# Weight pieces joined during attention, a third early unit, squares on another engine: one core of Trainium2

## The chip, the cores and the metric

The kernel runs on one core of a Trainium2 chip. The core has five engines with instruction queues of their own: TensorE (PE in the profile; its weight loads are PEld), VectorE (DVE), ScalarE (ACT), GpSimd (POOL) and SyncE (SP), which here only issues DMA transfers. Each engine works its queue strictly in order; semaphores tie the queues together. The metric is the device time of one launch in microseconds; lower is better. The inputs are float32 arrays in DRAM, and the output must agree with a float32 reference.

## The reference, cut to what matters

```python
# attention: batch 4, 12 heads, 448 positions, head size 64
scores = einsum('bhij,hg->bgij', (q @ k.T) / 8, w_pre)      # mix the heads
attn   = exp(scores - max); attn /= attn.sum() + 1e-9
out    = einsum('bhij,hg->bgij', attn, w_post) @ v          # mix the heads again
x = out as 1792 tokens x 768
h = ((x @ w1) * (x @ w2)) @ w3 @ w_out                      # 768 -> 1024 -> 1024 -> 768
h = relu(h @ w_in) ** 2 @ moe2_w_out                        # 768 -> 2048 -> 768
```

The weights reach the device as 64-bit words, two 32-bit halves for each element.

## The kernel before, in words

**Attention.** The scores are worked in 16 groups of query rows, cut into 180 blocks of up to 120 rows (10 queries times 12 heads). The loop of the main body runs over steps `d`, two blocks to a step. `attention_step` (L455) emits each step's work for each engine: premix (TensorE, line L295, tile `sp`), rowmax (VectorE, L301, `nm`), exp (ScalarE, L309), 1/sum, the high and the low fp16 part of the probabilities (L334 on ScalarE, L341 on VectorE, `ph` and `pl`), the second head mix one or two steps later (L351, `tp`), its copy out of PSUM (L364, L366, `p`), and the product with v (L392, `pv`). The scores of the next group (L269, `sc`) are worked in the same steps, up to step 82; the premix of the last two blocks is in step 89, the last two `pv` in step 92. SyncE regroups the rows of each block two steps ahead by DMA (`r<-s`, L287). The `sp` tile has two PSUM buffers, so a premix waits until exp has read the block two earlier.

**Weights.** A float32r matmul works on a high and a low part of weights and data, three matmuls to a product (`mm3`, L58). `Weights` holds the path of one piece (128 x 384 or 128 x 512). `load` is a DMA by SyncE, of 64-bit words ("wide", 384 KB for 384 columns) or of plain float32 (half of that). A wide piece then needs `narrow` (one ScalarE operation, L89) and `join` (three VectorE operations, L101, L103, L105), which make the float32 value `f`. Every piece needs `place`, `high` (ScalarE, L121) and `rest` (GpSimd or VectorE, L125), which make `wh` and `wl`. `keep` (L510) writes the joined float32 back to DRAM (`w1f` and so on), from ScalarE's DMA queue, since the second half of the tokens reads the same weights again.

**The layers after attention.** `Moe` runs the first 896 tokens (half 0, t = 0 and 1 of 448 tokens) by a list of units: 16 `l1` units (w1 and w2 by turns, two pieces each, L679), between the first 12 of them the 16 pieces of `w_out`, then `p34`, the last four `l1`, `ly`, `l3` (relu and square, L746) and `l4`. `stage` (L514) moves the pieces along, some places ahead of the unit that TensorE works. Half 1 (L1009) works by a product scheme with seven products for eight in `stream`, with `gate` and `square` (L990) as the ends of a stream, and between the streams the `y1` units and the `l4_1` units of two token blocks each. Its order is a list of events with planned times: a term that is planned at T + 3.6 is emitted then, and each engine's queue has the order of emission.

**Between the two.** At step 82 (`closed`) the pool of attention's first half is released. `tail_plan` (L540) hands out loads of x (L636, 0.7 MB each in rows of 880 or 912 bytes), their splitting (L644: ScalarE high, GpSimd low part), and the first eight pieces of w1 and w2, by block number from step 82 on; what is left over is emitted after the last step. `early` (L561) works t = 0 of the first two `l1` units in three PSUM banks that the scores leave, six groups of three matmuls each, one group at the very end of the loop (from block 187) and the rest behind it. Before, all 36 of these matmuls run behind the last `pv`.

Of the kernel before, what the change touches and what calls it, by code (L numbers as in the profile page):

```python
# [10 lines left out]
F = mybir.dt.float32  # L11
# [3 lines left out]
AF = mybir.ActivationFunctionType  # L15
# [11 lines left out]
PW = 512  # L27
# [8 lines left out]
def fused_kernel(ctx, tc, q, k, v, w_pre, w_post, w1, w2, w3t, wo, win, wo2, eye, out):  # L36
# [366 lines left out]
            eng.dma_start(xd[n // 4, :, 3 * y : 3 * y + 3, o : o + ic], u[:, :, :ic])  # L403


    TAIL = {"w": 5, "ws": 2, "w8": 13, "n": 4, "x": -1, "xs": 2, "xn": 4, "xt": 2, "h": 7, "hn": 1}

    def attention_plan():
        ev = {}

# [69 lines left out]


    class Moe:
        def __init__(self, wp):
            self.w = Weights(wp, PW, 4, 2, 4, 8, 8)
            self.wp = wp
            wp.tile([128, 24], F, tag="pad", name="pad")
            self.xy, self.acc, self.ready, self.serial = {}, {}, set(), 0
            self.wot = {}
            l1 = [self.l1(m, s) for m in range(8) for s in range(2)]
            wop = [self.wo_piece(c, h) for c in range(8) for h in range(2)]  # L490
            mixed, rest = l1[:4] + wop[:6], wop[6:]
            for i in range(8):
                mixed.append(l1[4 + i])
                for _ in range(1 + (i % 4 == 3)):
                    mixed.append(rest.pop(0))
            assert not rest
            self.units = mixed + [self.p34(m) for m in range(8)] + l1[12:]
            self.units += [self.ly(n) for n in range(6)]
            for gr in range(2):
                self.units += [self.l3(8 * gr + f) for f in range(8)]  # L500
                self.units += [self.l4(gr, e) for e in range(6)]
            self.pieces = [s for ss, *_ in self.units for s in ss]
            n = np.cumsum([0] + [len(ss) for ss, *_ in self.units])
            self.at = [int(x) for x in n]
            self.order = [(2, 0), (3, 0), (0, 1), None, (1, 1), None, (2, 1), None, (3, 1)]
            for i in range(10, len(self.units)):
                self.order += [(i, t) if self.units[i][1] else None for t in range(len(self.units[i][0]))]
            self.events, self.clock = [], -sum(self.units[it[0]][2] for it in self.order if it)

        def keep(self, i):  # L510
            if i in self.w.ft and self.pieces[i].get("keep") is not None:
# [28 lines left out]
        def tail_plan(self):  # L540

            w, ev = self.w, {}

            def at(t, f):
                ev.setdefault(t, []).append(f)

            for i in range(11):
                t = TAIL["w"] + TAIL["ws"] * i if i < 8 else TAIL["w8"] + i
                at(t, lambda i=i: w.load(i, self.pieces[i]["src"], self.pieces[i]["wide"]))
                if i < 9:  # L550
                    at(t + TAIL["n"], lambda i=i: w.narrow(i))
                if i < 8:
                    for part in range(3):
                        at(t + TAIL["n"] + 1 + part, lambda i=i, part=part: w.join(i, part))
                    at(t + TAIL["n"] + 4, lambda i=i: (w.place(i), w.high(i), self.keep(i), w.rest(i)))
            for u in range(4):
                at(TAIL["x"] + TAIL["xs"] * u, lambda u=u: self.load_x(u))
                at(TAIL["x"] + TAIL["xn"] + TAIL["xt"] * u, lambda u=u: self.split_x(u))
            return ev

        def early(self, i, psum):  # L561
# [10 lines left out]
        def begin(self, ap_):  # L572
            self.ap = ap_
            self.load_x(4)
            slots = []
            for i in range(3):
                t = self.six(1, f"wox{i}")
                slots += [t[:, c, :HC] for c in range(6)]
            slots += [ap_.tile([128, TB], R, tag="oa", name=f"woa{i}", bufs=12)[:, :HC] for i in range(12)]
            t = ap_.tile([128, HT], R, tag="bh", name="wob", bufs=8)  # L580
            slots += [t[:, :HC], t[:, TB : TB + HC]]
            for c in range(8):
                for h in range(2):
                    self.wot[c, h] = slots[4 * c + 2 * h], slots[4 * c + 2 * h + 1]
            for u in (5, 6, 7):
                self.load_x(u)
            for i in range(2):
                self.units[i][1](None, 0, slice(0, TB), self.acc[i])

        def run(self, ps):  # L590
# [155 lines left out]
        def l3(self, f):  # L746
            def run(ws, t, ts):
                yh, yl = self.xy["y", t]
                if t == 0:
                    self.xy["h", f] = self.big(f"h0_{f}")  # L750
                hb = self.xy["h", f]
                acc = self.psum(f"l3_0_{f}_{t}")
                mm3(acc, [(self.chunk(ws, c), (yh[:, c], yl[:, c])) for c in range(6)])

                def done():
                    r = self.tmp(f"r0_{f}_{t}")
                    nc.scalar.activation(r, acc, AF.Relu)
                    self.split_chain(hb, ts, r, (0.8, lambda: nc.vector.tensor_tensor(r, r, r, ALU.mult)))

                self.chain((3.6, done))  # L760

            return self.source("win", f, 0, HC), run, 3.6
# [227 lines left out]
        def square(self, f):  # L990
            def finish(q, block, z, bank):
                i = f + 2 * q + (block[1] == "2")
                ts = slice(0, TB) if block[2] == "1" else slice(TB, HT)
                if ("h1", i) not in self.xy:
                    self.xy["h1", i] = self.big(f"h1_{i}")
                dst = self.xy["h1", i]
                if bank is not None:
                    nc.scalar.activation(z, bank, AF.Relu)
                    self.split_chain(
                        dst, ts, z, (0.9, lambda: nc.gpsimd.tensor_tensor(z, z, z, ALU.mult)), (0.4, lambda: None)  # L1000
                    )
                else:
                    self.split_chain(
                        dst, ts, z, (0.7, lambda: nc.vector.scalar_tensor_tensor(z, z, 0.0, z, ALU.max, ALU.mult))
                    )

            return finish

        def half1(self):  # L1009
# [3 lines left out]
            D = {}  # L1013
            for n in (0, 3, 1, 4, 2, 5):
                ws = self.plain_weights(T, self.w34_source(n))
                for t in range(2):
                    def go(cs, n=n, t=t, ws=ws):
                        ts = slice(t * TB, t * TB + TB)
                        if 0 in cs:
# [32 lines left out]
                    self.event(T, lambda go=go: go(range(6)))  # L1052
                    self.event(T + 3.6, lambda go=go: go((6, 7)))
                    T += 4.8
                    self.event(T + 0.1, after)
            for gr in range(2):
                T = self.stream(
                    T, [(wf["win"][8 * gr + f], wf["win"][8 * gr + f + 1]) for f in range(0, 8, 2)],
                    lambda: D["y"], self.square(8 * gr), self.tmp,
                )  # L1060
                for e in range(6):
                    o = 1024 * gr
                    ws = self.plain_weights(T, [wf["wo2"][e, :, o + PW * i : o + PW * i + PW] for i in range(2)])
                    for t in range(2):
                        def go(cs, gr=gr, e=e, t=t, ws=ws):
                            ts = slice(t * TB, t * TB + TB)
                            if 0 in cs:
                                D["o", gr, e, t] = self.psum(f"l4_1_{gr}_{e}_{t}")
                            mm3(D["o", gr, e, t], [
                                (self.chunk(ws(), c), tuple(x[:, ts] for x in self.xy["h1", 8 * gr + c])) for c in cs  # L1070
                            ], 0 in cs, 7 in cs)

                        self.event(T, lambda go=go: go((0, 1, 2, 3, 4, 6)))
                        self.event(T + 3.6, lambda go=go: go((5, 7)))
                        T += 4.8
                        self.event(T + 0.1, lambda gr=gr, e=e, t=t: self.l4_out(D["o", gr, e, t], 1, gr, e, t))

    with tc.manual_schedule(), ExitStack() as base:
# [29 lines left out]
        A.setup_pre()  # L1108
        step = iter(range(-5, (first[16] + 5) // 2 + 2))
        closed = (first[15] - RG) // 2  # L1110
        M, tail = None, {}
        for d in step:
            attention_step(A, d, ev)
            if d == -1:
                A.setup_post()
            if d == closed:
                sa.close()
                M = Moe(pool(sa, "wp"))
                tail = M.tail_plan()
                heads = (x for i in range(2) for x in M.early(  # L1120
                    i, lambda i: ps.tile([128, TB], F, tag="sc", name=f"e{i}", bufs=3)
                ))
            for g in (2 * d, 2 * d + 1):
                for a in tail.pop(g - 2 * closed - 1, []):
                    a()
                for _ in range(TAIL["hn"] if g >= nb + TAIL["h"] else 0):
                    next(heads, None)
        for u in sorted(tail):
            for a in tail[u]:
# [61 lines left out]
```

## Time and profile before

| | before |
|---|---|
| median of three runs | 1346.34 us (1346.01 to 1347.26) |
| the profiled execution, device time | 1348.09 us |
| its span in the trace | 1346.3 us |
| busy in the span | PE 1296.7 us (96%), DVE 865.1 (64%), ACT 703.4 (52%), POOL 476.0 (35%) |
| mean granted TensorE clock | 0.985 |
| moved by DMA | 191 MB, 142 GB/s on the mean |

Attention takes the first 466 us of the span, half 0 the stretch to about 950 us (its end overlaps the start of half 1's preparation on VectorE), half 1 the rest. "Busy" is the time in which an engine executes; TensorE's matmuls overlap, so their durations in a timeline add up to more than their starts are apart. PEclk is the share of TensorE's full clock that was granted. A row of the waits view names who waited, for whom, how long in total, how often, and the longest.

### The profile page before, as it was taken

What the parts mean: (1) busy time and instruction counts of PE and PEld (TensorE: products, weight loads), DVE (VectorE), ACT (ScalarE), POOL (GpSimd) and SP (SyncE); (2) the same over time, 40 slices, a digit from 0 to 9 for tenths busy, and PEclk for the clock granted to TensorE, in tenths of its full rate; (3) what the DMA queues carried; (4) which work ended last, traced back from release to release, by engine and by line L of the source; (5) the groups of instructions that cost most, each with busy time, mean ns of one, the idle gap of its engine ahead of it and who ended that gap; (6) DMA issues with size and microseconds to landing.
All of it is one profiled execution on the core that took longest, in us unless ns stands there. A gap on an engine that the chain in (4) does not pass through costs nothing. (4 is left out here: it accounts for less than half of the span.)

```text
span 1346.3 us, 23524 instructions
## 1 busy us (share of the span) xinstructions
PE 1296.7 (96%) x8714; PEld 1120.9 (83%) x8714; DVE 865.1 (64%) x1446; ACT 703.4 (52%) x1518; POOL 476.0 (35%) x481
## 2 busy tenths in 40 slices
PE   6999999999998799899999999999999999899998
PEld 3677777777776688899999989989999999899988
DVE  4898788888787788865247884888254426602821
ACT  5878878878886455543223443444345335423520
POOL 4243253244222222101332232210588458624730
PEclk8999999999999799999999999999999999999989
DMA  6565476466545567765266764576211211220221
GB/s 187 169 185 176 135 212 184 130 184 197 139 125 170 151 197 213 214 196 162 73 188 189 240 198 148 131 232 213 96 47 56 79 55 48 68 74 25 71 71 58
DMA packets 106423, 191.31 MB, mean 142 GB/s; under 512 B 22021, under 2 KB 73221, under 8 KB 105861
## 3 DMA queue, kind: packets, MB, share of 16 engines
q1 hardware_dynamic: 86437, 167.42, 42.5%
q10 hardware_dynamic: 19872, 22.39, 4.7%
q8 instruction: 69, 1.13, 0.4%
q14 instruction: 45, 0.37, 0.1%
HBM read 115.46 MB, written 35.78 MB: 112 GB/s over the span
## 5 line engine op out<-in xcount | busy, mean ns | idle before, releaser
L125 POOL TENSOR_TENSOR wl<-f,wh 128x384 fp32r<-128x384 f32 (+1 forms) x76 | 84.3, 1110 | 298.4 <-ACT wh L121 282.7
L295 PE MATMUL sp<-r,kpre 120*120 120x448 f32 x360 | 158.6, 563 | 7.4 <-DMA r<-s 5.5
L309 ACT ACTIVATE p<-sp,nm 120x448 f32<-120x448 f32 x180 | 113.5, 638 | 69.9 <-DVE nm L301 69.0
L301 DVE TENSOR_REDUCE nm<-sp 120x1 f32<-120x448 f32 x180 | 108.1, 619 | 43.1 <-PE sp L295 36.8
L351 PEld LDWEIGHTS <-ph 120*128 120x128 f16 (+1 forms) x1440 | 107.9, 99 | 29.0 <-issue 28.5
L324 POOL TENSOR_SCALAR sm<-sm 120x2 f32<-120x2 f32 (+3 forms) x94 | 31.4, 334 | 273.8 <-ACT p L309 265.0
L351 PE MATMUL tp<-kwh,ph 120*128 120x120 f16 x720 | 121.4, 219 | 3.7 <-DVE p L366 2.4
L341 DVE SCALAR_TENSOR_TENSOR pl<-p,sm,ph 120x448 f16<-120x448 f32 x180 | 124.2, 730 | 0.0
L351 PE MATMUL tp<-kwh,pl 120*128 120x120 f16 x720 | 120.6, 218 | 1.0 <-DVE pl L341 1.0
L351 PE MATMUL tp<-kwl,ph 120*128 120x120 f16 x720 | 120.7, 218 | 0.0
L334 ACT ACTIVATE ph<-p,sm 120x448 f16<-120x448 f32 x180 | 111.8, 681 | 16.1 <-DVE sm L329 13.3
L269 PE MATMUL sc<-kt,qh 128*110 128x448 f32 (+1 forms) x192 | 101.3, 528 | 9.1 <-DVE kt L230 7.6
L295 PEld LDWEIGHTS sp<-r,kpre 120*120 120x120 f32 x360 | 59.0, 184 | 49.1 <-issue 21.5
L280 ACT ACTIVATE s<-sc 110x448 f32<-110x448 f32 (+1 forms) x186 | 90.2, 553 | 9.2 <-PE sc L269 7.5
L366 DVE TENSOR_SCALAR p<-tp,iv 112x480 f32<-112x480 f32 (+1 forms) x135 | 90.9, 701 | 3.0 <-PE tp L351 2.7
L121 ACT ACTIVATE wh<-f 128x384 fp32r<-128x384 f32 (+1 forms) x104 | 58.2, 559 | 60.5 <-DVE f L105 52.5
L101 DVE TENSOR_SCALAR f<-y 128x384 int32<-128x384 int32 (+1 forms) x120 | 71.7, 598 | 23.4 <-ACT y L89 23.4
L392 PE MATMUL pv<-p,v 112*64 112x110 f32 (+1 forms) x1536 | 84.9, 269 | 1.8 <-DVE p L366 1.2
L103 DVE SCALAR_TENSOR_TENSOR f<-y,f 128x384 int32<-128x384 int32 (+1 forms) x120 | 81.5, 679 | 4.0
L105 DVE SCALAR_TENSOR_TENSOR f<-raw,f 128x384 int32<-128x384 int32 (+1 forms) x120 | 79.9, 666 | 4.1
L392 PEld LDWEIGHTS pv<-p,v 112*64 112x64 f32 x1536 | 77.9, 142 | 5.3 <-ACT y L89 1.4
L269 PE MATMUL sc<-kt,ql 128*110 128x448 f32 (+1 forms) x192 | 75.1, 391 | 2.6 <-POOL ql L252 1.9
(981 smaller groups left out, 3522.2 us busy)
## 6 DMA issues: line engine op xcount, KB each, us to landing
r<-s SPq DMA_DIRECT2D x172, 210.0 KB
raw<-w SPq DMA_DIRECT2D x32, 384.0 KB
raw<-win SPq DMA_DIRECT2D x32, 384.0 KB
raw<-wo SPq DMA_DIRECT2D x24, 512.0 KB
kraw<-k SPq DMA_DIRECT2D x22, 448.0 KB
raw<-w3t SPq DMA_DIRECT2D x16, 512.0 KB
qraw<-q SPq DMA_DIRECT2D x36, 220.0 KB
raw<-wo SPq DMA_DIRECT2D x16, 384.0 KB
```

What stands on the lines that cost most here:

```text
L103: nc.vector.scalar_tensor_tensor(fi, yi, -0x80000000, fi, ALU.bitwise_and, ALU.bitwise_or)
L125: eng.tensor_tensor(self.out[i][1], self.ft.pop(i), f32(self.out[i][0]), ALU.subtract)
L269: nc.tensor.matmul(sc[:ic], t[:, hh * ic : hh * ic + ic], self.kt[b, h // 2][:, h % 2], start=(i == 0), stop=(i == 1))
L280: nc.scalar.activation(self.st[n][:ic, h], self.sc.pop((n, h))[:ic], AF.Copy)
L295: nc.tensor.matmul(t[:kk], self.kpre[:kk, :kk], self.rt.pop(g)[:kk], start=True, stop=True)
L301: nc.vector.tensor_reduce(nm[:kk], self.sp[g][:kk], AX.X, ALU.max, negate=True)
L309: nc.scalar.activation(p[:kk], self.sp.pop(g)[:kk], AF.Exp, bias=self.nm.pop(g)[:kk], accum_out=self.sm[g // 2][:kk, g % 2 : g % 2 + 1],)
L334: nc.scalar.activation(self.phl[g % NP][0][:kk, :S], self.pt[g][:kk], AF.Copy, scale=self.sm[g // 2][:kk, g % 2 : g % 2 + 1])
L341: nc.vector.scalar_tensor_tensor(l, self.pt.pop(g)[:kk], self.sm[g // 2][:kk, g % 2 : g % 2 + 1], h, ALU.mult, ALU.subtract)
L351: nc.tensor.matmul(t[:, j, :, :cnt], p[:kk, j * JP : j * JP + 128], w[:kk, :, :cnt], start=(i == 0), stop=(i == 2))
L366: nc.vector.tensor_scalar(d, t, self.iv[:JP], None, ALU.mult)
L392: nc.tensor.matmul(t[64 * e : 64 * e + 64, x, :ic], self.v[b][:, j, g], self.p2[n][:, j, g, :ic], start=(j == 0), stop=(j == JC - 1),)
```

## The change

Four things. (1) The `Moe` object is made before the loop. Its new method `ahead` takes the first 24 pieces that have a `keep` (all pieces of the first 12 `l1` units), and spreads their load, narrow, join and store over attention's steps: one piece every three steps from step 4, with two buffers for each kind of tile in attention's first pool; loads and stores are issued by SyncE. In the unit list these 24 pieces then are plain float32 from DRAM. (2) `tail_plan` is denser: loads of the first eight pieces one per block, x loads and splits one per block. `early` now works three units, one group per block from block 175 on, and the unit (2, 0) leaves the list. (3) The squares of `l3` (VectorE before) and of half 1's C21 block (GpSimd before) become a ScalarE `Square` behind the relu. (4) In half 1 the first `y1` unit and the first `l4_1` unit of each group work token block 1 ahead of block 0, and the two terms that are held back to T + 3.6 are chosen to match.

```diff
     class Moe:
-        def __init__(self, wp):
-            self.w = Weights(wp, PW, 4, 2, 4, 8, 8)
...
-            self.order = [(2, 0), (3, 0), (0, 1), None, (1, 1), None, (2, 1), None, (3, 1)]
+            self.order = [None, (3, 0), (0, 1), None, (1, 1), None, (2, 1), None, (3, 1)]
...
+        def ahead(self, ka, n, start, period):
+            w, ev = Weights(ka, PW, 2, 2, 2, 0, 0), {}
...
+            for j, i in enumerate([i for i, x in enumerate(self.pieces) if "keep" in x][:n]):
+                d, x = start + period * j, self.pieces[i]
+                at(d, lambda i=i, src=x["src"]: w.load(i, src, True))
+                at(d + 2, lambda i=i: w.narrow(i))
+                for part in range(3):
+                    at(d + 3 + part // 2, lambda i=i, part=part: w.join(i, part))
+                at(d + 6, lambda i=i, dst=x["keep"]: store(i, dst))
+                self.pieces[i] = {"src": x["keep"], "wide": False}
+            return ev
...
             for i in range(11):
-                t = TAIL["w"] + TAIL["ws"] * i if i < 8 else TAIL["w8"] + i
+                t = 1 + i if i < 8 else 13 + i
                 at(t, lambda i=i: w.load(i, self.pieces[i]["src"], self.pieces[i]["wide"]))
-                if i < 9:
-                    at(t + TAIL["n"], lambda i=i: w.narrow(i))
+                if i == 8:
+                    at(t + 4, lambda i=i: w.narrow(i))
                 if i < 8:
-                    for part in range(3):
-                        at(t + TAIL["n"] + 1 + part, lambda i=i, part=part: w.join(i, part))
-                    at(t + TAIL["n"] + 4, lambda i=i: (w.place(i), w.high(i), self.keep(i), w.rest(i)))
+                    at(t + 4, lambda i=i: (w.place(i), w.high(i), w.rest(i)))
             for u in range(4):
-                at(TAIL["x"] + TAIL["xs"] * u, lambda u=u: self.load_x(u))
-                at(TAIL["x"] + TAIL["xn"] + TAIL["xt"] * u, lambda u=u: self.split_x(u))
+                at(u - 1, lambda u=u: self.load_x(u))
+                at(u + 3, lambda u=u: self.split_x(u))
...
                 def done():
                     r = self.tmp(f"r0_{f}_{t}")
                     nc.scalar.activation(r, acc, AF.Relu)
-                    self.split_chain(hb, ts, r, (0.8, lambda: nc.vector.tensor_tensor(r, r, r, ALU.mult)))
+                    nc.scalar.activation(r, r, AF.Square)
+                    self.split_chain(hb, ts, r)
...
                     nc.scalar.activation(z, bank, AF.Relu)
-                    self.split_chain(
-                        dst, ts, z, (0.9, lambda: nc.gpsimd.tensor_tensor(z, z, z, ALU.mult)), (0.4, lambda: None)
-                    )
+                    nc.scalar.activation(z, z, AF.Square)
+                    self.split_chain(dst, ts, z)
...
-                for t in range(2):
+                held = []
+                for t in ((1, 0) if n == 0 else (0, 1)):
...
-                    for t in range(2):
+                    for t in ((1, 0) if e == 0 else (0, 1)):
...
-                        self.event(T, lambda go=go: go((0, 1, 2, 3, 4, 6)))
-                        self.event(T + 3.6, lambda go=go: go((5, 7)))
+                        late = (5, 7) if t == 0 else (4, 6)
+                        self.event(T, lambda go=go, late=late: go([c for c in range(8) if c not in late]))
+                        self.event(T + 3.6, lambda go=go, late=late: go(late))
...
+        M, tail = Moe(), {}
+        ahead = M.ahead(ka, 24, 4, 3)
         for d in step:
             attention_step(A, d, ev)
+            for a in ahead.get(d, ()):
+                a()
...
-                heads = (x for i in range(2) for x in M.early(
+                heads = (x for i in range(3) for x in M.early(
...
-                for _ in range(TAIL["hn"] if g >= nb + TAIL["h"] else 0):
+                for _ in range(1 if g >= nb - 5 else 0):
                     next(heads, None)
```

## Rows read from the trace of the kernel before

**Rows 1.** Windows view, stretches: length, busy us of each engine (instructions), clock, DMA.
```profile
66.80:120.40 53.60, 53.46 (x570) 39.80 (x569) 49.38 (x86) 42.79 (x103) 23.61 (x28) 1.00 0.61 184
...
294.60:321.40 26.80, 26.11 (x269) 18.80 (x266) 24.32 (x46) 21.01 (x50) 15.30 (x17) 1.00 0.59 185
53.40:401.80 348.40, 346.45 (x3657) 257.29 (x3656) 293.76 (x549) 283.34 (x673) 118.81 (x154) 1.00 0.57 165
```
**Rows 2.** Windows view of later stretches: PE, PEld, DVE, ACT, POOL, clock, DMA.
```profile
475.00:575.00 100.00, 92.94 (x452) 84.28 (x453) 87.67 (x162) 52.77 (x105) 18.31 (x18) 0.98 0.72 209
750.00:950.00 200.00, 195.97 (x971) 181.20 (x970) 149.60 (x228) 88.29 (x175) 45.49 (x40) 1.00 0.62 194
1150.00:1300.00 150.00, 143.79 (x687) 131.89 (x686) 59.18 (x77) 54.12 (x108) 77.33 (x64) 0.97 0.19 60
441.00:456.60 15.60, 11.00 (x124) 8.57 (x125) 14.75 (x26) 8.92 (x20) 5.00 (x6) 0.76 0.57 142
```
**Rows 3.** Windows view, short stretches with a lowered clock, the same columns.
```profile
565.00:569.00 4.00, 4.00 (x16) 4.00 (x15) 3.90 (x8) 1.21 (x2) 0.00 (x0) 0.57 0.71 240
1172.00:1177.00 5.00, 4.47 (x14) 4.04 (x15) 0.48 (x1) 1.58 (x3) 2.14 (x2) 0.66 0.17 57
1285.00:1293.00 8.00, 7.43 (x21) 6.33 (x22) 1.71 (x2) 1.84 (x5) 3.61 (x4) 0.57 0.34 94
```
**Rows 4.** Waits view of PE, 475 to 600 us: total us, times, longest.
```profile
PE p L62 <- DVE wl L125: 3.2, 1, 3.2
```
**Rows 5.** Waits of PE, 1150 to 1300 us.
```profile
PE l L62 <- ACT bhh L965: 3.9, 4, 1.4
PE l L62 <- DVE blh L966: 2.3, 4, 0.6
```
**Rows 6.** Groups of DVE instructions, 475 to 575 us: count, busy us, mean ns.
```profile
L105 DVE SCALAR_TENSOR_TENSOR f<-raw,f 128x384 int32<-128x384 int32 x32 | 22.1, 689 | 1.1
L103 DVE SCALAR_TENSOR_TENSOR f<-y,f 128x384 int32<-128x384 int32 x32 | 19.5, 608 | 1.1
L101 DVE TENSOR_SCALAR f<-y 128x384 int32<-128x384 int32 x32 | 11.2, 351 | 0.0
```
**Rows 7.** Timeline of PE at attention's end: start, us, what, idle before.
```profile
422.43 1.82 PE L295 MATMUL sp<-r,kpre 120*120 120x448 f32 x4 [1.98 <-DMA r<-s]
...
432.83 1.76 PE L295 MATMUL sp<-r,kpre 120*120 120x448 f32 x4 [1.32 <-DMA r<-s]
...
440.98 2.22 PE L295 MATMUL sp<-r,kpre 108*108 108x448 f32 x4 [1.69 <-ACT p L309]
...
445.84 2.48 PE L392 MATMUL pv<-p,v 112*64 112x110 f32 x48
...
456.62 4.99 PE L392 MATMUL pv<-p,v 112*64 112x118 f32 x48 [1.21 <-DVE p L366]
462.17 4.50 PE L392 MATMUL pv<-p,v 112*64 112x118 f32 x48 [0.56 <-ACT xs L401]
...
474.83 0.48 PE L62 MATMUL l<-xh,wh 128*128 128x448 f32 x1 [0.76 <-ACT a L691]
```
**Rows 8.** Timeline of SP's queue: one of the x loads.
```profile
423.94 0.58 SPq L642 DMA_DIRECT2D xl<-xd  x1
```
**Rows 9.** Timeline of DVE: the low parts of two steps.
```profile
419.76 1.27 DVE L341 SCALAR_TENSOR_TENSOR pl<-p,sm,ph 120x448 f16<-120x448 f32 x2
...
424.83 2.11 DVE L341 SCALAR_TENSOR_TENSOR pl<-p,sm,ph 120x448 f16<-120x448 f32 x2
```
**Rows 10.** Timeline of POOL: one low part of x.
```profile
424.27 1.59 POOL L650 TENSOR_TENSOR xl<-xl,xh 128x660 fp32r<-128x660 f32 x1 [3.18 <-ACT xh L648]
```
**Rows 11.** Instructions of line 758: ns min/median/max, first and last start.
```profile
L758 DVE TENSOR_TENSOR r<-r x32: 615/618/626, 722.8 to 903.0; 128x448 f32<-128x448 f32 x32
```
**Rows 12.** Timeline of POOL before the second l4 group of half 1: a square.
```profile
1283.18 1.31 POOL L1000 TENSOR_TENSOR 6.4000000000002_3P<-6.4000000000002_3P 128x448 f32<-128x448 f32 x1
```
**Rows 13.** Timeline of ACT at the start: the table load.
```profile
0.73 1.28 ACT L247 ACT_TABLE_LOAD   x1 [0.73 <-PEq L1146]
```

More of the change, by code (lines that the diff above doesn't have):

```diff
@@ L403, in pv_out @@
             eng.dma_start(xd[n // 4, :, 3 * y : 3 * y + 3, o : o + ic], u[:, :, :ic])
-    TAIL = {"w": 5, "ws": 2, "w8": 13, "n": 4, "x": -1, "xs": 2, "xn": 4, "xt": 2, "h": 7, "hn": 1}
     def attention_plan():
@@ L482, in fused_kernel, with __init__ @@
     class Moe:
-        def __init__(self, wp):
-            self.w = Weights(wp, PW, 4, 2, 4, 8, 8)
-            self.wp = wp
-            wp.tile([128, 24], F, tag="pad", name="pad")
+        def __init__(self):
             self.xy, self.acc, self.ready, self.serial = {}, {}, set(), 0
@@ L508, in __init__, with at, store, open @@
             self.events, self.clock = [], -sum(self.units[it[0]][2] for it in self.order if it)
+        def ahead(self, ka, n, start, period):
+            w, ev = Weights(ka, PW, 2, 2, 2, 0, 0), {}
+            def at(d, f):
+                ev.setdefault(d, []).append(f)
+            def store(i, dst):
+                nc.sync.dma_start(dst, w.ft[i])
+            for j, i in enumerate([i for i, x in enumerate(self.pieces) if "keep" in x][:n]):
[7 more added lines that the diff above has]
+            return ev
+        def open(self, wp):
+            self.w = Weights(wp, PW, 4, 2, 4, 8, 8)
+            self.wp = wp
+            wp.tile([128, 24], F, tag="pad", name="pad")
         def keep(self, i):
@@ L586, in begin @@
                 self.load_x(u)
-            for i in range(2):
+            for i in range(3):
                 self.units[i][1](None, 0, slice(0, TB), self.acc[i])
@@ L1054, in half1 @@
                     T += 4.8
-                    self.event(T + 0.1, after)
+                    held.append(after)
+                    if n:
+                        self.event(T + 0.1, after)
+                if n == 0:
+                    self.event(T + 0.1, held[1])
+                    self.event(T + 0.2, held[0])
             for gr in range(2):
@@ L1070, in go @@
                                 (self.chunk(ws(), c), tuple(x[:, ts] for x in self.xy["h1", 8 * gr + c])) for c in cs
-                            ], 0 in cs, 7 in cs)
-                        self.event(T, lambda go=go: go((0, 1, 2, 3, 4, 6)))
-                        self.event(T + 3.6, lambda go=go: go((5, 7)))
+                            ], 0 in cs, 0 not in cs)
+                        late = (5, 7) if t == 0 else (4, 6)
+                        self.event(T, lambda go=go, late=late: go([c for c in range(8) if c not in late]))
+                        self.event(T + 3.6, lambda go=go, late=late: go(late))
                         T += 4.8
@@ L1110, in fused_kernel @@
         closed = (first[15] - RG) // 2
-        M, tail = None, {}
+        M, tail = Moe(), {}
+        ahead = M.ahead(ka, 24, 4, 3)
         for d in step:
             attention_step(A, d, ev)
+            for a in ahead.get(d, ()):
+                a()
             if d == -1:
@@ L1117, in fused_kernel @@
                 sa.close()
-                M = Moe(pool(sa, "wp"))
+                M.open(pool(sa, "wp"))
                 tail = M.tail_plan()
-                heads = (x for i in range(2) for x in M.early(
+                heads = (x for i in range(3) for x in M.early(
                     i, lambda i: ps.tile([128, TB], F, tag="sc", name=f"e{i}", bufs=3)
```

## Prediction, made blind

> **What bounds the kernel now.** I read the busy shares first, then the windows view in 50 us slices, then TensorE's waits by stage, and last the timelines of the stretches where it waits. TensorE is busy for 1296.7 of 1346.3 us, and no edit takes matmuls away, so only its idle time and its slow clock can be won. The windows say where these are. In 53 to 402 us, which is most of attention, TensorE idles for 348.4 - 346.45 = 2 us [rows 1]: nothing to win, and all the new work of `ahead` goes there. The other places are attention's last steps (422 to 475 us), the first l1 units (475 to 575 us, 7.1 us idle), l3 and l4 of half 0 (750 to 950 us, 4.0 us) and the two entries into `l4_1` in half 1 (1150 to 1300 us, 6.2 us) [rows 2]. Behind three of them the clock was granted at 0.57 to 0.66 of full for some microseconds [rows 3], each time after TensorE had stood idle.
>
> **1. Joins inside attention.** A join is three VectorE operations, 351 + 608 + 689 ns = 1.65 us [rows 6]; 24 of them are 39.6 us. VectorE is busy for 293.8 of 348.4 us there [rows 1], so 54.6 us are free and the work fits on the mean (93 to 96% busy). It doesn't fit everywhere. At a batch's change VectorE also casts k: in 66.8 to 120.4 us it is busy for 49.38 of 53.6 us, and four joins make that 55.98, 2.4 us too much; in 294.6 to 321.4 us 24.32 + 3.3 = 27.62 of 26.8, 0.8 too much [rows 1]. There are three such changes; I give the third the smaller price. Behind the joins the next rowmax is queued, behind that exp, and behind exp the premix that wants its PSUM buffer, so an excess reaches TensorE: +2.4 + 0.8 + 0.8 = **+4 us**. Ends: 0, if the queues' play takes it (no gain is possible, since nothing leaves this stretch), and +39.6, if every join goes on the path. I stay near the lower end because the excess is worked out from the fullest rows.
>
> The other parts of a piece I cost at nothing there. Narrow is one ScalarE operation of some 0.55 us behind a step's own work, 13 us in all, and ScalarE has 65 us free [rows 1]. Load and store put 24 x (384 + 192 KB) = 14 MB through SyncE, some 42 GB/s beside 165, so the DMA share goes from 0.57 to about 0.72 [rows 1]. They are issued behind the regroupings of their own step and ahead of the next step's, which are wanted two steps on. That cover would be gone if a regrouping landed a whole step late, and each time would then cost what the waits for `r` at the end cost, 1.3 to 2.0 us [rows 7].
>
> **2. Attention's end.** The last premix starts at 440.98, the first of the last two pv at 456.62, the main l1 at 474.83 [rows 7]. The unit (2, 0), 3.6 us, still follows there and is an early one after the change, so the moment to compare is 478.4.
>
> What is late before 440.98: two premixes wait 1.98 and 1.32 us for `r` [rows 7], each behind one of the two x loads in the DMA queue, the second issued at 423.94 [rows 8]. The change issues that load one step earlier, so its wait only moves to an earlier premix. What it adds: loads of pieces 4 to 7 now stand in SyncE's queue ahead of the last two pairs of regroupings, and must wait for a `raw` buffer, which is free when GpSimd's rest of pieces 0 to 3 is done; that waits for ScalarE's high part at the end of a step. So the last regroupings go out later. I take +2.5 us for the last premix (0 to +5): between no wait and two and a half waits as long as the longest row for `r`.
>
> From there: in 441.0 to 456.6 us TensorE works for only 11.0 us at a clock of 0.76, about 8 us of work at full clock, and VectorE is busy for 14.75 of 15.6 us [rows 2], some 6 us of it joins (three to four times 1.65 us [rows 6]). Without these VectorE needs 9.7 us. TensorE gets six early groups there (three matmuls of 0.2 us each; the 36 before took 474.83 - 0.76 - 466.67 = 7.4 us [rows 7]), 3.7 us, and so 11.9 us: it now sets the pace, and stands idle little. So I expect full clock for the last two pv: 2.48 us each, as the one at 445.84, instead of 4.99 and 4.50 [rows 7]. Nine groups (5.6 us) stay behind them. Sum: 441.0 + 2.5 + 11.9 + (2.48 + 0.56 + 2.48) + 5.6 + 0.8 for the change of PSUM pools = 467.3, against 478.4: **-11 us**. Ends: -17 with no delay of the last premix and VectorE's 9.7 us alone on the path, -2 with five microseconds of delay and the pv still at half clock.
>
> Here a row and a page meet. The low parts of two blocks took 1.27 us alone and 2.11 us when GpSimd's 1.59 us subtraction of x lay beside them [rows 9, 10]. The Trainium skill (SBUF — State Buffer, "SBUF: two separate sides") says why: an operation of VectorE with two SBUF inputs and a GpSimd operation exclude each other for their whole length. This speaks against the change in two places: two of a join's three operations have two inputs, and GpSimd is busy for 34% of attention (118.8 of 348.4 us), 44% at the first batch change [rows 1]. By the rule, 48 operations that meet such an operation one time in three, and wait half of some 1.1 us, are 9 us more on VectorE; half of that on the path makes part 1 +8 instead of +4, and the time 4 us longer. The joins priced in rows 6 were beside GpSimd work too, so I leave the sum as it is.
>
> **3. First l1 units.** TensorE idles for 7.1 us in 475 to 575 us [rows 2], 3.2 of them at one wait for a low part of w_out from VectorE [rows 4], and then runs 3.4 us at half clock (0.57 over 4 us [rows 3]), 1.7 us lost. VectorE, busy for 87.7 of 100 us [rows 2], loses the joins of 16 pieces, 26 us. It keeps the 16 pieces of w_out and the ends of the l1 units, at about 60%. What is late next is a high part on ScalarE, which still waits for the joins of w_out. I take **-7.5** of the 8.8 us (ends -4 and -8.8).
>
> **4. Squares of l3.** 32 VectorE operations of 618 ns go [rows 11] and 32 on ScalarE come, which is busy for 88 of 200 us [rows 2]; relu, square and high part stand in one queue, with a hop to VectorE and back less. Hidden, but for the entries into l4, where TensorE idles for 4.0 us in all [rows 2]. Part of that is low parts of weights, which stay: **-2.5** (0 to -4).
>
> **5. Entries into l4 of half 1.** 6.2 us idle [rows 2], all of it for the last h1 chunks [rows 5]; and 3.4 and 6.9 us at half clock behind them (1 - 0.66 over 5 us, 1 - 0.57 over 8, twice) [rows 3], half of which is lost: 5.1 us. Block 1 first puts 4.8 us between the last product of the stream and the terms that need it, and its chain loses GpSimd's 1.31 us [rows 12]. The longest wait was 1.4 us [rows 5]. So both go: **-11** of 11.3 (ends -8, if block 1's own held-back terms are late by half a wait, and -11.3). The `y1` units show no wait before; 0.
>
> **Sum** on the profiled execution: +4 - 11 - 7.5 - 2.5 - 11 = -28, so 1348.1 - 28 = 1320.1. That execution is 1.75 us over the median of the runs (1346.34), so I forecast **1318.3**.
>
> **Rivals.**
> (a) VectorE becomes attention's bound. Place: the step in which two thirds of a join stand ahead of the next rowmax. If TensorE waits out every join, the price is 39.6 us, against 32 won elsewhere: 1346.3 + 7.6 = 1354. It decides from 32 / 24 = 1.33 us a piece, 80% of a join. For it: 49.4 of 53.6 us busy [rows 1]. Against: 54.6 us free over the whole. Chance 0.06.
> (b) Attention's end gives little: regroupings late and pv at half clock (-2), while the joins meet GpSimd and cost 10 us. With parts 3 to 5 at -7, -2.5, -11: -12.5, so 1334. For it: the longer DMA queue and GpSimd's rests, moved into these steps. Against: VectorE loses 6 us of 15.6. Chance 0.2.
> (c) All goes well: part 1 at 0, part 2 at -17, the rest at its ends: -41, 1305. Chance 0.05.
> (d) The squares don't do what they say: the trace has one table load, 1.28 us [rows 13], before all copies, exps and relus. If Square is not in that table, each of 40 squares needs a load to and back, 102 us on ScalarE. Those of l3 would mostly hide in 112 us of idle ScalarE [rows 2]; the 8 in half 1 stand at the two entries, 8 x 2.56 = 20 us: 1338. The Trainium skill (ScalarE: Activation LUTs, "Table sets: the hidden batching unit") says that cheap functions are in every set; it doesn't list Square among them. Chance 0.02.
> The forecast keeps 0.67; its own range is 1309 to 1328.
>
> **Range and chances.** 1308 to 1335 takes in the forecast and most of (b), and leaves out (a), (d) and most of (c). A measurement of this kernel tells about 0.2% from no change, 2.7 us. Faster 0.67 + 0.2 + 0.05 + 0.02, less a reserve for worse ends of (b): 0.91. Slower 0.06. Same 0.03.
>
> **What would show it.** Part 1: idle time of TensorE in 66 to 120 us of about 2.5 us, released by exp or rowmax, and VectorE at 93% or more. Part 2: main l1 starting about 467 + 4 (for part 1), the last pv at 2.5 us each, full clock. Part 3: no wait of p34 for VectorE. Part 4: entries into l4 without a wait for `bhh`. Part 5: no idle and no lowered clock in the two entries. Wrong would make it: a wait of premix for `r` or for exp in every third step; half clock at the last pv; table loads in ScalarE's rows.

## The result, and the profile after

| | before | after |
|---|---|---|
| median, runs | 1346.17 us, 4 (1345.94 to 1347.26) | 1330.18 us, 4 (1325.54 to 1333.60) |
| ratio | | 0.9877 [0.9844, 0.9911] |
| the same again, later | 1347.02 us, 7 | 1331.33 us, 4 (1328.39 to 1333.05), 0.9880 [0.9862, 0.9897] |
| profiled execution, span | 1348.09, 1346.3 us | 1333.60, 1331.7 us |

The change saves 16 us, where 28 were forecast: 1330.2 against 1318.3, inside the range of 1308 to 1335 but beyond the forecast case's own 1309 to 1328. The direction was right; one term was mis-sized by far.

The windows view of the kernel after, in the stretches that answer to [rows 1, 2] (the later ones shifted by as much as their work was; columns as there):
```profile
53.40:401.80 348.40, 334.39 (x3465) 244.84 (x3464) 307.80 (x586) 276.76 (x656) 116.44 (x147) 0.99 0.67 197
66.80:122.00 55.20, 52.60 (x550) 38.54 (x549) 53.00 (x96) 44.04 (x105) 24.96 (x28) 1.00 0.68 208
494.00:594.00 100.00, 98.07 (x498) 92.42 (x498) 72.59 (x127) 46.59 (x92) 17.37 (x17) 0.98 0.53 155
755.00:955.00 200.00, 200.00 (x1002) 187.48 (x1001) 135.86 (x203) 103.18 (x196) 45.89 (x40) 1.00 0.60 190
1145.00:1295.00 150.00, 150.00 (x752) 140.61 (x751) 59.48 (x81) 61.75 (x122) 76.79 (x63) 1.00 0.21 66
```
The last three lines are what was hoped for: TensorE idles for 1.9 us in the first l1 units, where it idled for 7.1, and works without a gap through l3, l4 and the two entries of half 1, where it idled for 4.0 and 6.2 us. The first line is what was not: in the first 350 us of the loop TensorE idles for 14.0 us, where it idled for 2.0, and it issues 3465 matmuls where it issued 3657.

In the timeline of TensorE, the premix of block 168 (step 84) is a mark that stands behind all of ahead's work and in front of nearly all of attention's changed end. Before it:
```profile
417.42 1.76 PE L295 MATMUL sp<-r,kpre 120*120 120x448 f32 x4
```
and after:
```profile
436.60 1.76 PE L295 MATMUL sp<-r,kpre 120*120 120x448 f32 x4
```
The same matmul is 19.2 us later. The few loads of the changed end that go out before it did not delay it: in no_ahead below, which has them too, it starts at 416.69. With more such marks, each the same matmul in both traces, the difference of the spans comes apart like this (time after less time before at the mark; what the stretch up to it gave):

| up to | before, after | difference | the stretch | forecast |
|---|---|---|---|---|
| premix of block 168 | 417.42, 436.60 | +19.2 | **+19.2** | +4 |
| the unit (3, 0) of l1 | 478.54, 489.54 | +11.0 | **-8.2** | -11 |
| p34 | 607.05, 611.83 | +4.8 | **-6.2** | -7.5 |
| behind l4's second entry, half 0 | 909.36, 907.99 | -1.4 | **-6.2** | -2.5 |
| the last matmul | 1342.06, 1327.79 | -14.3 | **-12.9** | -11 |

### The profile page after: what moved, and what is told of

Read it like the earlier page. It is cut to its first block, busy times and chain, and to the rows that moved or that the text cites. A ratio compares the mean times of both kernels' runs of the same rounds, so it can differ in the third digit from the quotient of the medians.

```text
span 1331.7 us, 23506 instructions
## 1 busy us (share of the span) xinstructions
PE 1291.6 (97%) x8714; PEld 1117.5 (84%) x8714; DVE 839.9 (63%) x1414; ACT 727.0 (55%) x1558; POOL 469.6 (35%) x473
## 4 chain that ended last, share of the span: by engine, by line
PE 75%; issue 7%; ACT 6%; DVE 5%; DMA 4%; POOL 3%; SPq 0%; POOLq 0%; ACTq 0%; DVEq 0%
PE l L62 33%; PE y L62 9%; PE p L62 5%; PE sp L295 4%; PE tp L351 3%; PE pv L392 3%; ACT p L309 3%; PE sc L269 2%; DMA kraw<-k 1%; ACT ph L334 1%; POOL ql L252 1%; DVE p L366 1%; ACT s L280 1%; DVE nm L301 1%; POOL sm L324 1%
## 5 line engine op out<-in xcount | busy, mean ns | idle before, releaser
L295 PE MATMUL sp<-r,kpre 120*120 120x448 f32 x360 | 163.1, 575 | 14.1 <-ACT p L309 7.2
L125 POOL TENSOR_TENSOR wl<-f,wh 128x384 fp32r<-128x384 f32 (+1 forms) x52 | 58.6, 1127 | 215.0 <-ACT wh L121 205.4
L103 DVE SCALAR_TENSOR_TENSOR f<-y,f 128x384 int32<-128x384 int32 (+1 forms) x120 | 85.6, 713 | 4.1
L392 PE MATMUL pv<-p,v 112*64 112x110 f32 (+1 forms) x1536 | 80.7, 261 | 0.6 <-ACT xs L401 0.6
L392 PEld LDWEIGHTS pv<-p,v 112*64 112x64 f32 x1536 | 73.8, 137 | 4.0 <-ACT xs L401 0.8
L125 POOL TENSOR_TENSOR wl<-raw,wh 128x384 fp32r<-128x384 f32 (+1 forms) x36 | 44.2, 1231 | 92.1 <-ACT wh L121 92.1
```

The source lines that it names most:

```text
L125: eng.tensor_tensor(self.out[i][1], self.ft.pop(i), f32(self.out[i][0]), ALU.subtract)
L295: nc.tensor.matmul(t[:kk], self.kpre[:kk, :kk], self.rt.pop(g)[:kk], start=True, stop=True)
L392: nc.tensor.matmul(t[64 * e : 64 * e + 64, x, :ic], self.v[b][:, j, g], self.p2[n][:, j, g, :ic], start=(j == 0), stop=(j == JC - 1),)
```

## The experiments

| kernel | median us (lowest to highest) | ratio to before, interval |
|---|---|---|
| no_ahead | 1313.01 (1311.33 to 1315.92) | 0.9748 [0.9734, 0.9763] |
| dma_only | 1318.99 (1316.58 to 1319.61) | 0.9787 [0.9773, 0.9802] |
| join_only | 1323.26 (1321.90 to 1326.13) | 0.9825 [0.9810, 0.9840] |
| squares_order | 1328.25 (1326.27 to 1333.03) | 0.9860 [0.9836, 0.9884] |
| order_only | 1333.98 (1331.64 to 1334.84) | 0.9894 [0.9870, 0.9918] |
| tail_spaced | 1325.43 (1322.87 to 1329.37) | 0.9837 [0.9814, 0.9860] |
| tail_loads_late | 1328.80 (1326.56 to 1330.42) | 0.9854 [0.9835, 0.9872] |
| quiet_16 | 1322.81 (1321.28 to 1324.60) | 0.9815 [0.9797, 0.9833] |
| quiet_16_spaced | 1318.37 (1316.35 to 1325.30) | 0.9793 [0.9767, 0.9819] |
| quiet_14_spaced | 1318.73 (1317.09 to 1320.88) | 0.9787 [0.9765, 0.9809] |
| quiet_8_spaced | 1322.99 (1321.43 to 1323.37) | 0.9815 [0.9796, 0.9835] |

Each ratio is to runs of the kernel before in the same set. no_ahead, dma_only and join_only leave out all or a part of ahead's work, so their times price that work; in these three both halves read the pieces from q.

**What in ahead costs 19 us?** Four kernels on one chip.

> The changed kernel once more, beside the three that follow, since its four runs lay 8 us apart (1325.5 to 1333.6). Every theory: 1325 to 1334, and a spread of some microseconds again.

It was 1331.33 us, with a spread of 4.7 us.

> The changed kernel without any work of ahead in attention: the 24 pieces are read as plain float32 from the array q (so their values are not the weights), and everything behind is unchanged. The premix of block 168 came 19.2 us later than before in the changed kernel. Theory V (VectorE's queue) and theory D (DMA traffic and SyncE's queue) both say that all of it goes: 1330 - 19 = 1311, 1307 to 1314. If the delay came from elsewhere (another layout of the pools, say), 1325 or more.

```diff
-                at(d, lambda i=i, src=x["src"]: w.load(i, src, True))
-                at(d + 2, lambda i=i: w.narrow(i))
...
-                at(d + 6, lambda i=i, dst=x["keep"]: store(i, dst))
-                self.pieces[i] = {"src": x["keep"], "wide": False}
+                self.pieces[i] = {"src": q[j % 4, :, HC * (j // 4) : HC * (j // 4) + HC], "wide": False}
```

> Ahead only loads and stores (its narrow and joins are left out; the 24 pieces are read from q as in no_ahead). V: within 3 us of no_ahead, since VectorE has nothing more to do. D: 10 to 19 us above no_ahead.

> Ahead only narrows and joins (on two pieces that are loaded once and used again; no other load, no store; the pieces are read from q). V: 14 to 19 us above no_ahead, with idle time of TensorE released by exp. D: within 3 us of no_ahead.

The change without ahead's work took 1313.0 us: 18.3 less than with it. That is also what the forecast comes to without its part 1 (1318.3 - 4 = 1314.3), so by the sum all of the miss lies in that part; the misses of the other four (+2.8, +1.3, -3.7 and -1.9 us in the table above) nearly cancel. The transfers alone cost 6.0 us, the joins alone 10.3, both 18.3. Neither theory was right by itself: V said at most 3 for the transfers, D at most 3 for the joins.

How transfers cost TensorE time can be looked for in VectorE's waits. The waits of VectorE in 53.4 to 401.8 us, no_ahead:
```profile
DVE qh L245 <- DMA qraw<-q: 6.8, 9, 1.3
DVE kt L221 <- DMA kraw<-k: 4.6, 4, 1.5
```
and dma_only:
```profile
DVE qh L245 <- DMA qraw<-q: 11.3, 9, 1.9
DVE kt L221 <- DMA kraw<-k: 8.5, 7, 2.8
```
VectorE stands 8.4 us longer in front of casts whose q or k has not landed, with the next rowmax queued behind them. TensorE's waits there, dma_only:
```profile
PE sp L295 <- ACT p L309: 2.6, 3, 1.4
PE sp L295 <- DMA r<-s: 1.9, 3, 1.3
PE sp L295 <- ACT s L280: 1.2, 2, 0.8
```
Late regroupings, the case that I had looked at, make 1.9 us of this, and 1.2 us are put down to ScalarE's copies of the scores; 2.6 us are waits for exp, which needs the rowmax that stands in VectorE's in-order queue. That the transfers cause these 2.6 is not shown. The trace of order_only (below) has none of these transfers, and in the same stretch it has:
```profile
PE sp L295 <- ACT p L309: 2.5, 2, 1.5
DVE qh L245 <- DMA qraw<-q: 8.3, 8, 2.5
DVE kt L221 <- DMA kraw<-k: 4.8, 2, 2.5
```
So the way by q, k and VectorE's queue is argued. Without ahead, TensorE's waits for a regrouping are 0.3 us at most (no_ahead). With the joins alone:
```profile
PE sp L295 <- ACT p L309: 4.8, 7, 1.8
PE sc L269 <- POOL ql L252: 2.2, 9, 0.4
```
and in the change itself:
```profile
PE sp L295 <- ACT p L309: 6.5, 9, 2.1
PE sp L295 <- DMA r<-s: 2.7, 2, 1.8
PE sc L269 <- POOL ql L252: 2.3, 8, 0.4
PE sp L295 <- ACT s L280: 0.7, 1, 0.7
```
A premix that waits for exp waits for a rowmax that came late. The second of the two waits for `r`, 1.77 us in step 67, was followed by half clock, and over steps 66 to 71 the change lost 4.0 us against no_ahead, where either part alone lost at most 0.6. Step by step, the premix of join_only falls back against no_ahead by 7.8 us from step 8 to step 80, and some 7 of it in steps 8 to 20, 32 to 41 and 59 to 61, around the three changes of batch, as forecast for them, but with nearly twice the size. Another 2.5 us arose before step 8, and no work of ahead is shown to cause them: the premix of step 8 starts at 57.30 in no_ahead's trace, at 59.81 in join_only's, and at 59.71 to 60.10 in those of the kernel before, squares_order and order_only, which have no ahead. Counted from step 8 to step 80, the trace of dma_only falls back by 5.0 us, join_only by 7.8, and the change by 17.6 (15.9 in after_again); kernels without ahead lie between -2.1 and +0.6.

**Does joining in attention pay?** The kernel before with only the squares and the order:

> The kernel before with the squares on ScalarE and the new order in half 1 alone: no ahead, the old end of attention with two early units. From the traces, l3 and l4 of half 0 gave 6.2 us and the entries of half 1 gave 12.9 us, so 1346.5 - 19.1 = 1327.4. Theory N (joining in attention doesn't pay: it costs 18 us there and returns 14 in attention's end and in l1): 1326 to 1329, no slower than the whole change. Theory P (it pays: l3 gained only because VectorE was ahead): 1333 or more.

```diff
                     nc.scalar.activation(r, acc, AF.Relu)
-                    self.split_chain(hb, ts, r, (0.8, lambda: nc.vector.tensor_tensor(r, r, r, ALU.mult)))
+                    nc.scalar.activation(r, r, AF.Square)
+                    self.split_chain(hb, ts, r)
...
-                        self.event(T, lambda go=go: go((0, 1, 2, 3, 4, 6)))
-                        self.event(T + 3.6, lambda go=go: go((5, 7)))
+                        late = (5, 7) if t == 0 else (4, 6)
```

1328.25 us, ratio 0.9860 [0.9836, 0.9884]: no slower than the whole change. Theory N holds: as made, ahead and the denser end take about as much as they give. Of the two parts, order_only undoes the squares again:

> The kernel before with the new order of blocks in half 1 alone, squares as before. Theory O (the order makes the room, the squares are needed for l3 only): the two entries give 12 to 13 us, l3 nothing: 1334. Rival (GpSimd's square is what was late): the entries give half, 1340.

1333.98 us; theory O. Its windows view, in the stretches of [rows 2]:
```profile
1150.00:1300.00 150.00, 150.00 (x751) 140.61 (x751) 60.26 (x79) 54.72 (x109) 79.50 (x66) 1.00 0.23 71
750.00:950.00 200.00, 195.96 (x971) 181.16 (x970) 149.30 (x228) 88.39 (x175) 45.90 (x40) 1.00 0.62 193
```
With GpSimd's squares still there the entries have no gap (751 matmuls, 687 before), and l3 is as before to a matmul (971). So the order gave all of the 12.9 us, and the squares the 6.2 us in l3 and l4 of half 0, nothing else.

**Attention's end.**

> The changed kernel with the loads of the first eight pieces at attention's end one every two blocks instead of every block (and place, high and rest with them). Theory S (SyncE waits for a raw buffer ahead of the last regroupings, and GpSimd's two rests in a step stand ahead of the sums): the last premix 3 to 5 us earlier, 1325 to 1328 against 1331. Rival (the end is bound by the x loads and by TensorE's own work): within 1 us of 1331.

```diff
-                t = 1 + i if i < 8 else 13 + i
+                t = 1 + 2 * i if i < 8 else 13 + i
```

> The changed kernel with the loads of pieces 4 to 7 behind the last regrouping, pieces 0 to 3 as they are. If SyncE's wait is what delays the last premix, as in tail_spaced (3 to 5 us of it). If it is GpSimd's doubled rests, about half of that, since four pieces still come two to a step.

```diff
-                t = 1 + i if i < 8 else 13 + i
+                t = 1 + i if i < 4 else 7 + i if i < 8 else 13 + i
```

1325.43 and 1328.80 us against 1331.33. As ratios these are 0.9837 and 0.9854 against 0.9880 [0.9862, 0.9897], so the second is not clear of the change. The timeline of SyncE's queue in the change:
```profile
443.13 0.96 SPq L81 DMA_DIRECT2D raw<-w2f  x2
444.19 2.63 SPq L287 DMA_DIRECT2D r<-s  x2
450.83 3.62 SPq L81 DMA_DIRECT2D raw<-w1f  x2
454.54 1.69 SPq L287 DMA_DIRECT2D r<-s  x2
459.97 1.31 SPq L81 DMA_DIRECT2D raw<-w2f  x2
461.37 1.73 SPq L287 DMA_DIRECT2D r<-s  x2
```
and in tail_spaced:
```profile
442.71 1.69 SPq L287 DMA_DIRECT2D r<-s  x2
444.45 0.50 SPq L81 DMA_DIRECT2D raw<-w2f  x1
445.83 1.68 SPq L287 DMA_DIRECT2D r<-s  x2
447.57 0.49 SPq L81 DMA_DIRECT2D raw<-w2f  x1
448.22 1.72 SPq L287 DMA_DIRECT2D r<-s  x2
```
The last pair of regroupings goes out at 461.37 behind two loads that wait for a buffer, instead of 448.22. In tail_loads_late the last six go out one behind another, with no load between them:
```profile
442.27 6.38 SPq L287 DMA_DIRECT2D r<-s  x6
```
The sums of the softmax stand behind GpSimd's two rests in a step; GpSimd in the change:
```profile
458.57 2.35 POOL L125 TENSOR_TENSOR wl<-raw,wh 128x384 fp32r<-128x384 f32 x2 [2.56 <-ACT wh L121]
461.01 0.19 POOL L324 TENSOR_SCALAR sm<-sm 120x2 f32<-120x2 f32 x1
```
and VectorE behind it:
```profile
461.24 0.17 DVE L329 RECIPROCAL sm<-sm 120x2 f32<-120x2 f32 x1 [2.16 <-POOL sm L324]
```
From the premix of block 168 to the unit (3, 0) it took 61.1 us before, 52.9 in the change (52.7 to 52.9 in the five other traces with the same end), 51.4 in tail_loads_late and 49.8 in tail_spaced. SyncE's wait is not what holds the last premix: in tail_loads_late, where the last regroupings have gone out 14 us behind the premix of block 168 (the last pair in the change begins at 24.8), the last premix comes 27.9 us behind it, as in after_again (27.9; 28.5 in the change's first trace), and 25.8 in tail_spaced. What is left is the doubled rests, for which the expectation had about half the gain, as measured; no kernel changes them alone. The medians of the change and tail_spaced differ by 5.9 us, more than that stretch's 3.1; what the rest is, these traces do not show.

**Where to put the joins.**

> Sixteen pieces instead of 24 in attention, one join operation to a step, and only in steps without casts of k (5 to 8, 18 to 29, 40 to 51, 63 to 80, counted by the joins). Theory K (the loss is at the batch changes, where VectorE has no room): part 1 costs 3 to 5 us instead of 18, l1 gives back some 2 us: 1317 to 1321. Rival (each piece costs the same wherever it lies, 0.75 us): 12 us instead of 18, and 1326 to 1328.

```diff
-            for j, i in enumerate([i for i, x in enumerate(self.pieces) if "keep" in x][:n]):
-                d, x = start + period * j, self.pieces[i]
+            quiet = [3, 6] + list(range(18, 28, 3)) + list(range(40, 50, 3)) + list(range(63, 79, 3))
+            for j, i in enumerate([i for i, x in enumerate(self.pieces) if "keep" in x][:n]):
+                d, x = quiet[j] - 3, self.pieces[i]
...
-                    at(d + 3 + part // 2, lambda i=i, part=part: w.join(i, part))
-                at(d + 6, lambda i=i, dst=x["keep"]: store(i, dst))
+                    at(d + 3 + part, lambda i=i, part=part: w.join(i, part))
+                at(d + 7, lambda i=i, dst=x["keep"]: store(i, dst))
...
-        ahead = M.ahead(ka, 24, 4, 3)
+        ahead = M.ahead(ka, 16, 4, 3)
```

1322.81 us, 8.5 below the change; a little less than theory K said, and well beyond its rival. The edit changes three things at once, the number of pieces, the steps and one operation to a step; which of them gave how much was not tried. The three kernels that follow add the spacing of tail_spaced.

> quiet_16 with the spaced loads of tail_spaced. If the two gains are of different stretches they add: 1322.8 - 4.5 = 1318, 1316 to 1320. If SyncE's wait was late only because the joins had delayed everything, 1321 to 1323.

> The same without the two pieces in steps 0 to 10: 14 pieces. In quiet_16's trace the premix of block 168 was 5.8 us later than in no_ahead, of which only 0.9 us arose behind step 4: if the two early loads cause the rest, 1314 to 1316; if it is a low clock in the first 50 us that comes and goes from run to run, 1318 to 1320, as quiet_16_spaced.

> Only the eight pieces that attention's end needs, in steps without casts of k; the other 16 are joined in l1 as before, where they cost 2 to 4 us (from the first main l1 to p34 it took 82.0 us before, 79.7 after). Theory: 2 to 3 us above quiet_14_spaced. Rival: VectorE in l1 is free enough, and each piece left out of attention saves 0.1 to 0.7 us: the same or faster.

1318.37, 1318.73 and 1322.99 us. The two gains add. The two early pieces make no difference, so the time of that expectation's other case holds. Its reason fits in part: in 0 to 53.4 us the mean granted clock was 0.94 in quiet_16's trace, and 1.00 in those of quiet_16_spaced and quiet_14_spaced. Eight pieces are 4 us worse than 16 or 14, where 2 to 3 were expected: what the other pieces cost in l1 is more than what they cost in quiet steps. From the unit (3, 0) to p34 it took 132.8 us with eight pieces and 124.0 in quiet_16_spaced. TensorE's waits in 53.4 to 401.8 us, quiet_16_spaced:
```profile
PE sp L295 <- ACT p L309: 1.9, 3, 1.2
PE sp L295 <- DMA r<-s: 1.4, 4, 0.7
```
Its ratio to before is 0.9793 [0.9767, 0.9819], where the change's is 0.9877 [0.9844, 0.9911]: with quiet_14_spaced the fastest found of the kernels that leave no work out, some 12 us faster than the change. In its trace the premix of block 168 starts at 421.88, in no_ahead's at 416.69; 3.2 of these 5.2 us arose before step 8, where the other kernels without ahead are 2.4 to 2.8 us behind no_ahead's trace too. So some 2 us behind step 8 are what attention pays for 16 pieces in this trace.

## Why the prediction was right or wrong

**Part 1 failed, by its size.** The step that failed is the excess for joins of 4 us together with "The other parts of a piece I cost at nothing there". The joins alone cost 10.3 us and the transfers alone 6.0; together 18 to 19. The loss lies between the ends that I gave, 0 and 39.6, and the place, the changes of batch, held for the joins: in 66.8 to 122 us TensorE idles for 2.6 us, where about 2.5 was said. I stayed too near the lower end.

Three things were left out. The sum took whole stretches of 27 and 54 us, in which free time of VectorE in one step makes up for another; but a step is some 4.7 us, and free time that has gone by is not had again. quiet_16 fits this, but does not test it alone. The cover for the transfers was looked for at the regroupings alone, while q and k are loaded just a step ahead of casts on VectorE, the engine without room; the price of 6.0 us is measured, its way to TensorE is not. And a mean price of a join hides where the long ones lie, as the next paragraph shows. Whether joins and transfers make each other worse is open: the medians give 16.3 us apart and 18.3 together, which is within the intervals, and the traces behind step 8 give 12.8 apart and 15.9 to 17.6 together.

The Trainium skill (SBUF — State Buffer, "SBUF: two separate sides") says that an operation of VectorE with two SBUF inputs and a GpSimd operation that reads SBUF exclude each other: whichever starts first holds the port for its whole length. The trace agrees: such an operation that lay beside one of GpSimd took up to 1.51 us, where the median is 0.55. By this rule I had worked out 9 us more on VectorE and left them out of the sum. Joins in attention, groups of VectorE in 53.4 to 401.8 us of the change:
```profile
L105 DVE SCALAR_TENSOR_TENSOR f<-raw,f 128x384 int32<-128x384 int32 x23 | 16.6, 723 | 0.0
L103 DVE SCALAR_TENSOR_TENSOR f<-y,f 128x384 int32<-128x384 int32 x23 | 15.3, 665 | 0.8
L101 DVE TENSOR_SCALAR f<-y 128x384 int32<-128x384 int32 x23 | 8.4, 366 | 0.0
```
723 + 665 + 366 = 1.75 us a join, where 1.65 was taken [rows 6]: 2.5 us in 24 joins. That is the mean. The same operations by their shortest, median and longest time in ns:
```profile
L105 DVE SCALAR_TENSOR_TENSOR f<-raw,f x23: 546/551/1512, 66.9 to 395.1; 128x384 int32<-128x384 int32 x23
L103 DVE SCALAR_TENSOR_TENSOR f<-y,f x23: 557/559/1391, 62.5 to 391.5; 128x384 int32<-128x384 int32 x23
```
Nine of these 46 took 0.89 to 1.51 us, 6.4 us in all over the median, and each of the nine lay beside a low part of k or q on GpSimd. The longest, on VectorE and on GpSimd:
```profile
96.73 1.51 DVE L105 SCALAR_TENSOR_TENSOR f<-raw,f 128x384 int32<-128x384 int32 x1
96.64 2.60 POOL L230 TENSOR_TENSOR kt<-kraw,kt 64x448 fp32r<-64x448 f32 x2
```
They fell in steps 14, 15, 33, 39, 56, 57, 62, 63 and 69, and join_only's trace has nine in the same steps. Some 5 us of what it lost against no_ahead lie in steps with such an operation or up to three steps behind one, and 2.8 us in steps 18 to 20 and 60 without one (at step 60 squares_order and order_only, which have no joins there, lost 1.0 and 1.1 too). So the long operations have a share in the loss at the changes of batch. How much TensorE paid for them, beside the lack of room, no run separates: quiet_16 avoids both, but for two such operations, 0.7 us over the median.

**Part 2 held for the last pv, not for the delay.** -8.2 us for -11. The timeline of TensorE in the change, to be read beside [rows 7]:
```profile
442.55 3.31 PE L295 MATMUL sp<-r,kpre 120*120 120x448 f32 x4 [2.92 <-DMA r<-s]
...
465.11 0.92 PE L295 MATMUL sp<-r,kpre 108*108 108x448 f32 x2
...
478.25 2.64 PE L392 MATMUL pv<-p,v 112*64 112x118 f32 x48
481.46 2.64 PE L392 MATMUL pv<-p,v 112*64 112x118 f32 x48 [0.57 <-ACT xs L401]
...
492.94 0.36 PE L62 MATMUL l<-xh,wl 128*128 128x448 f32 x1
493.80 0.47 PE L62 MATMUL l<-xh,wh 128*128 128x448 f32 x1 [0.50 <-ACT xh L665]
495.74 0.44 PE L62 MATMUL l<-xl,wh 128*128 128x448 f32 x1 [1.47 <-DVE xl L667]
```
The last two pv run at full clock, 2.64 us each for 4.99 and 4.50, as forecast. The last premix came 28.5 us after block 168's, 23.6 before: 4.9 later, where +2.5 was taken and +5 was the end. The reason that I gave, regroupings that go out late, was not the one that counted: tail_loads_late sends them earlier and gains 0.6 us at most, tail_spaced, which also sets the rests apart, 2.7 (25.8).

**Part 3** gave -6.2 for -7.5. p34's wait for VectorE fell from 3.2 to 0.4 us; new are 2.0 us in front of the second unit's x (the two rows at 493.80 and 495.74), which is loaded and split late, and a half-clock stretch behind them.

**Parts 4 and 5** gave more than forecast, 6.2 and 12.9 for 2.5 and 11. In part 4 I had set the whole prize at 4.0 us, TensorE's idle time. The counts of matmuls in equal stretches give it rightly: 971 and 1002 in 200 us are 31 matmuls of 0.2 us, 6.2 us; 687 and 752 in 150 us are 13.0, idle time and half clock together [rows 2]. The row of before alone could have told it, since 200 us hold 1000 such matmuls. A matmul that starts behind a gap is shown as busy for longer (0.47 us at 493.80, 0.36 at 492.94), and hides some of the loss.

**The rivals.** (b) came nearest in its sum (1334 against 1330): transfers and joins cost more than its 10 us, attention's end gave more than its 2. (a) did not come: 18 us of 39.6. (c) did not: part 1 was not at 0. (d) did not: l3 and half 1 show no gap, and the change's trace has one table load, of 1.28 us, as before.

## What to carry to other kernels

Work that fits an engine on the mean need not fit in a loop whose every step has that engine on its path: sum it by step, with the steps that are already full taken out, and put the work into the others, one small operation to a step. Look at the longest instance of an operation beside its mean, and at what the other engines did then. Price transfers that are added to a stretch by a run of their own: here they cost 6 us where nothing was set down. And before a second engine's idle time is called free, price the work with and without it: here the part that looked like the change's core returned nothing until it was moved.

## What the runs showed of the hardware that was not expected

Half-clock stretches also came in the middle of attention: the profile after has waits of 2.13 us at 184 us and of 1.77 us at 356 us, and behind each some 3.4 us at half clock. In 184 to 190 us the mean granted clock was 0.72:
```profile
184.00:190.00 6.00, 5.79 (x40) 4.17 (x42) 5.92 (x10) 4.84 (x13) 4.30 (x4) 0.72 0.71 231
```
Not every such wait was followed by one: after_again waits 1.82 us at 316 and again at 354 us, and its mean clock in 53.4 to 401.8 us is 1.00. The runs of the change spread over 8 us, those of the kernel before over 1.3 us beside them, though over 4 to 7 us in later sets. squares_order, which has no new work in attention, spreads as far (1326.27 to 1333.03), so the joins are not needed for it. Whether such stretches make the spread was not tried.
